# A spectral and state-space network on one core: long convolutions in quarter tiles of TensorE, the complex products summed by TensorE

## The chip, the cores and the metric

The kernel runs on one core of one Trainium2 chip. The metric is device time in microseconds. TensorE multiplies matrices and is recorded as PE, with its weight loads apart as PEld; VectorE is DVE, ScalarE is ACT, GpSimd is POOL, and SyncE (SP) mostly issues DMAs. Inputs, outputs and arithmetic are float32, except a few bfloat16 products that build the convolution kernels.

## The reference

Four layers with residuals on x of 1 x 2048 x 512, A, B, A, B; A filters with a 2-D FFT, B is a causal convolution over the 2048 positions with one kernel K per channel:

```python
def _A_ref(x, w_r, w_i):
    return irfft2(rfft2(x) * (w_r + 1j * w_i), s=(2048, 512))

def _B_ref(u, ...):
    dt = exp(log_dt); A = -exp(log_A_real) + 1j * A_imag; C = (C_real + 1j * C_imag) * dt[:, None]
    K = 2 * einsum("dn,dnl->dl", C, exp((A * dt[:, None])[:, :, None] * arange(2048))).real
    y = irfft(rfft(u.T, 4096) * rfft(K, 4096), 4096)[:, :2048].T
    return y + u * D_skip

x = x + _A_ref(layernorm(x)); x = x + _B_ref(layernorm(x)); x = x + _A_ref(layernorm(x)); x = x + _B_ref(layernorm(x))
```

The kernels K and their spectra are the same for both B layers.

## The kernel before

A B layer works in four blocks of 128 channels. For each block:

- `forward_b.rows` (four calls): the input's first Fourier stage. TensorE multiplies 64x64 pieces with a table T of twiddles; ACT copies the two banks to the tile z (L651).
- `turn` (eight calls): DVE transposes z in 32x32 pieces (L657), so that the position within a residue lies across partitions.
- `pair(i)` (four calls): the second stage. The weights are a matrix `mb` of 128 rows that is block-diagonal over two sets of channels, so half of each product is with zeros. It gives two planes, the real and the imaginary part.
- `weigh(i)`: the complex product with K's spectrum, two tiles `kk` of 128x512 per i. DVE makes four real products of 128x512 from PSUM into `wb` (L963), a small one mends frequency zero (L965), and four sums of 64x512 bring them together in the tile Y (`u`, L975). The strings YB and YC give each sum to POOL ("g") or DVE ("v").
- `back.units` (eight calls, four for each half j of Y): Y is the weight and MBT the moving operand, 16 products each; ACT copies to V (L988). The first call of each half also mixes frequency zero (L983, L984).
- `back.rows` (four calls): the last stage, 8 products each, and DVE adds the residual (L1002).

`kernel_time` builds K in time order for 32 channel groups (exponentials and sines on ACT, products on DVE at L840, L859 and L861, small products on TensorE at L872, a copy on ACT at L879 and stores `kt<-stage` at L883). `kernel_freq` then sends K through the same forward stages and keeps the spectrum in `kk` tiles, stored to memory (L938). The first B layer takes these tiles from SBUF directly (`kept`); the second loads them back (L957).

The order is written out by hand: lists of steps for one block, the next block's forward stages, K's build (`fill`) and the layer's tail are interleaved by position, and the framework's scheduler then sets each engine's stream. Each engine runs its stream in order. All matrix products of a group go through the helper `side_by_side`, whose one line is L319, and `mb`, `t` and `u` name the operands. In the first B layer PSUM has two banks for p1 and p3 together and three for p2 until K is built (`PM`), then five and three (`PB`); in the second two, three and three.

## Time and profile before

| what | value |
|---|---|
| median of 3 runs | 785.22 us (782.49 to 788.17) |
| profiled execution | 786.58 us, span 784.8 us |
| PE busy | 612.4 us, 8208 instructions |
| DVE busy | 646.6 us, 1301 instructions |
| ACT busy | 420.4 us |
| POOL busy | 415.4 us |
| moved by DMA | 80.26 MB |

A float32 product is two records in PE and two in PEld, so 64 products show as x128. From 120 us to 460 us the kernel builds K, beside the end of the first A layer and most of the first B layer; to about 540 us the rest of that layer runs; then the second A layer, and from 679 us the products of the second B layer.

### The profile page before, as it was taken

The page shows a single profiled execution, that of the slowest core. Times are in us where ns is not written, and L with a number is a line of the kernel's source. Part 1 is how long each engine was busy: PE and PEld are TensorE (multiplying, and loading weights), DVE is VectorE, ACT ScalarE, POOL GpSimd, SP SyncE. Part 2 cuts the span into 40 slices and gives each one's busy share as a digit, 9 for nine tenths or more (in the row PEclk, how much of TensorE's full clock was granted, in tenths as well). Part 3 has the DMA queues.
Part 4 walks back from the last instruction along what each step waited for, and adds up shares of the span by engine and source line. Part 5 has one row for each costly group of instructions (what it writes and reads, how often), then busy time and mean ns, then how long its engine had stood idle before and what let it go on. Part 6 is the DMA issues. An engine that isn't in the chain of part 4 may idle for free. (4 is left out here: it accounts for less than half of the span.)

```text
span 784.8 us, 20886 instructions
## 1 busy us (share of the span) xinstructions
PE 612.4 (78%) x8208; PEld 417.6 (53%) x8208; DVE 646.6 (82%) x1301; ACT 420.4 (54%) x919; POOL 415.4 (53%) x596
## 2 busy tenths in 40 slices
PE   3337788698758687897867977865899897889986
PEld 2336566464424342654343645644877664466666
DVE  7999749889997769968996977878587598789993
ACT  3434788755556676787477833323766335243322
POOL 3675886766625226732675166281055473375850
PEclk9656999998975999899989999997999898799998
DMA  8300651343547232452326359422122004134403
GB/s 320 117 0 1 147 124 49 102 101 129 125 161 148 72 105 49 129 139 79 43 67 146 113 120 252 133 82 81 54 82 83 28 14 147 56 91 128 145 24 105
DMA packets 144257, 80.26 MB, mean 102 GB/s; under 512 B 78656, under 2 KB 123840, under 8 KB 143264
## 3 DMA queue, kind: packets, MB, share of 16 engines
q1 hardware_dynamic: 143904, 78.51, 36.0%
q8 instruction: 65, 1.06, 0.5%
q0 software_dynamic: 256, 0.43, 0.3%
q14 instruction: 32, 0.26, 0.1%
HBM read 54.30 MB, written 25.03 MB: 101 GB/s over the span
## 5 line engine op out<-in xcount | busy, mean ns | idle before, releaser
L975 POOL TENSOR_TENSOR u<-wb,wb 64x512 f32<-64x512 f32 x90 | 137.0, 1523 | 81.2 <-DVE wb L963 74.5
L319 PE MATMUL p<-z,mb 128*64 128x512 f32 (+1 forms) x480 | 104.0, 543 | 13.2 <-DVE wb L963 5.8
L651 ACT COPY z<-p 128x512 f32<-128x512 f32 x96 | 51.5, 595 | 70.5 <-PE p L319 47.0
L861 DVE TENSOR_TENSOR qp<-qp,mag 128x1024 f32<-128x1024 f32 x64 | 83.3, 1305 | 1.2
L963 DVE TENSOR_TENSOR wb<-p,kk 128x512 f32<-128x512 f32 x128 | 80.6, 674 | 4.0 <-PE p L319 4.0
L859 DVE SCALAR_TENSOR_TENSOR qp<-qp,mag 128x256 f32<-128x256 f32 x128 | 63.6, 512 | 18.7 <-ACT qp L805 18.4
L319 PEld LDWEIGHTS p<-mb,u 128*64 128x64 f32 x2048 | 67.6, 146 | 17.9 <-issue 9.6
L319 PE MATMUL p<-mb,u 128*64 128x64 f32 x2048 | 69.9, 231 | 8.6 <-DVE u L975 4.2
L657 DVE STREAM_TRANSPOSE z<-z 128x512 f32<-128x512 f32 x96 | 58.5, 673 | 21.1 <-ACT z L651 21.1
L1087 POOL TENSOR_SCALAR w<-w,norms 128x128 f32<-128x128 f32 x64 | 37.8, 604 | 62.7 <-DMA w<-h 59.7
L530 DVE TENSOR_TENSOR w<-wt,p 128x514 f32<-128x514 f32 x64 | 42.5, 687 | 32.4 <-PE p L319 24.2
L535 POOL TENSOR_TENSOR w<-w,w 64x257 f32<-64x257 f32 x48 | 40.0, 834 | 53.7 <-DVE w L530 45.8
L872 PEld LDWEIGHTS pv<-qp 128*32 128x32 f32 x2048 | 38.0, 120 | 53.8 <-issue 20.2
L805 ACT ACTIVATE kf<-pk 128x512 f32<-128x512 f32 x64 | 38.8, 606 | 48.7 <-PE pk L841 48.4
L459 PE MATMUL p<-w,w 128*128 128x128 f32 x128 | 32.1, 429 | 40.6 <-DVE w L452 30.9
L319 PEld LDWEIGHTS p<-z,mb 128*64 128x64 f32 x480 | 34.4, 142 | 50.5 <-issue 30.9
L319 PE MATMUL p<-t,w 64*64 64x128 f32 x1024 | 48.1, 309 | 16.7 <-DMA w<-kt 8.1
L872 PE MATMUL pv<-qp 128*32 128x64 f32 x2048 | 51.6, 240 | 8.2 <-DVE qp L861 5.3
L988 ACT COPY u<-p 128x512 f32<-128x512 f32 x64 | 37.4, 589 | 38.1 <-PE p L319 38.1
L840 DVE TENSOR_SCALAR kw<-pk 128x512 bf16<-128x512 f32 x64 | 43.0, 679 | 13.3 <-PE pk L839 13.3
L319 PEld LDWEIGHTS p<-t,w 64*64 64x64 f32 x1024 | 36.8, 152 | 29.0 <-DMA w<-kt 10.7
L459 PEld LDWEIGHTS p<-w,w 128*128 128x128 f32 x128 | 27.8, 318 | 44.6 <-issue 24.7
(198 smaller groups left out, 1498.1 us busy)
## 6 DMA issues: line engine op xcount, KB each, us to landing
wt<-in_w SPq DMA_DIRECT2D x32, 257.0 KB
kf<-kk SPq DMA_DIRECT2D x32, 256.0 KB
kk<-kf SPq DMA_DIRECT2D x32, 256.0 KB
u<-in_x SPq DMA_DIRECT2D x16, 256.0 KB
hr<-in_x SPq DMA_DIRECT2D x16, 256.0 KB
kt<-stage SPq DMA_DIRECT2D x32, 128.0 KB
h<-hr SPq DMA_DIRECT2D x16, 256.0 KB
w<-kt SPq DMA_DIRECT2D x32, 128.0 KB
```

The source lines that it names most:

```text
L319: last = self.nc.tensor.matmul(out, weights, data, start=not more, stop=True, skip_group_check=True).ins
L459: nc.tensor.matmul(p[:, b], xf[:, b], t, start=True, stop=True)
L530: nc.vector.tensor_mul(m[pl], W, px[:, None, :].to_broadcast([128, 2, 257]))
L535: e[0].tensor_sub(Y[0:64, v], m[0][hs, 0], m[1][hs, 1])
L651: nc.scalar.copy(tiles["z"][:, :, :, b, m:m + 2].rearrange("p u j m r -> p (u j) (m r)"), ps[b].rearrange("p u j m r -> p (u j) (m r)"))
L657: nc.vector.transpose(tiles["zt"][:, u:u + 8].rearrange("p u j d -> p (u j d)"), tiles["z"][:, u:u + 8].rearrange("p u j b m r -> p (u j b ...
L840: nc.vector.tensor_scalar(whole, p, MAGIC, -MAGIC, op0=ALU.add, op1=ALU.add)
L859: nc.vector.scalar_tensor_tensor(QP[:, c, 0], QP[:, c, 1, :, ::-1], -1.0 if c else 1.0, m[:, 0], op0=ALU.mult, op1=ALU.mult)
L861: nc.vector.tensor_mul(t, t, mag[:, None, 1:3, 256 * j:256 * j + 256].to_broadcast([128, 2, 2, 256]))
L872: nc.tensor.matmul(p[32 * t:32 * t + 32, g], QP[:, c, 2, d], QP[:, c, 0:2, d], start=c == 0, stop=c == 1, tile_position=(0, 32 * t), skip_ ...
L963: nc.vector.tensor_mul(split(m[c, pl], "du", [32, 16]), by_channel(p), split(k[c], "du", [32, 16]))
L975: self.added = e[0].tensor_sub(y[0:64], v[0, 0], v[1, 1]), e[1].tensor_add(y[64:128], v[0, 1], v[1, 0])
```

## The change

- The channels of a block are split once more, into four sets of 32 (j, q). z has two sets in its lower 64 partitions and two in its upper, and every product of the convolution has 64 rows. `forward_b.rows` has 32 products of 64x32 weights instead of 16 of 64x64; `pair` has four products of 64x64 weights per kind, with no zeros; `units` is called four times, with two banks and 32 products for each plane M; `rows` is called twice, with two banks and 64 products of 64 columns.
- With ADD false (first B layer) DVE's four products per i go straight into two tiles M (`u`), times the spectrum's real part and times its imaginary part; nobody adds them. TensorE sums them in `units`, the second with turned weights (MT). With ADD true (second B layer) `pair` makes two kinds, one with turned weights (TWI); DVE makes four products per i into `wb`, and POOL adds them in two sums of 128x512 into one M.
- The spectrum is needed on other partitions: `weigh` loads four tiles per i, each in two DMAs that read every row twice, in both layers. Only the last block of the first B layer takes it from SBUF, with weights DUP. POOL copies frequency zero into the loaded tiles.
- M is a single set, written by a block's four `weigh` and read by its four `units`. `mix` comes once per block.
- DQ gives the stores `kt<-stage` and `kf<-kk` to ACT's queue instead of SP's. `stage` has one buffer instead of two, `qp` four instead of five, and LAGV is 3 instead of 4. `xw` has one buffer of twice the size.

```diff
@@ -19,14 +19,14 @@
-WW = 8
-DQ = ''
+WW = 6
+DQ = 'TaUa'
-LAGV = 4
+LAGV = 3
...
@@ -50,12 +50,13 @@
-QP = 5
+QP = 4
-WB = 7
-YB = 'vgggvggg'
-YC = 'vgggvgggvgvgvgvv'
+WB = 5
+ADD = False, True
+XW = 1
+WX = 11
...
@@ -638,13 +652,19 @@
                 tiles["z"] = self.sb("z", [64, 2, 2, 8, 2])
             xs = [src(n0 + i) for i in range(4)]
             ps = [self.ps("p1", [64, 2, 2, 2]) for b in range(2)]
...
+            products = []
+            e = extra() if extra and n0 == 0 else None
+            for m in range(2):
+                for j in range(2):
+                    for q in range(2):
+                        for c in range(2):
+                            for b in range(2):
+                                o = ps[b][64 * q + 32 * c:64 * q + 32 * c + 32, :, j, m]
+                                t = T[64 * b:64 * b + 64, n0 + 2 * m + c].rearrange("p (u r) -> p u r", r=2)
+                                d = slice(64 * j + 32 * q, 64 * j + 32 * q + 32)
+                                products.append((o, xs[2 * m + c][64 * b:64 * b + 64, d], t))
+                                if e is not None and m == c == b == 0:
+                                    products.append((o, e[:, d], t, True))
             self.side_by_side(products)
             m = n0 // 2
             for b in range(2):
@@ -657,23 +677,33 @@
             nc.vector.transpose(tiles["zt"][:, u:u + 8].rearrange("p u j d -> p (u j d)"),
                                 tiles["z"][:, u:u + 8].rearrange("p u j b m r -> p (u j b m r)"))
...
+        def pair(i, use, kinds):
+            z = tiles["zt"]
             last = None
...
+            for x, K in enumerate(kinds):
+                ps = [self.ps("p2", [512]) for q in range(2)]
                 products = []
...
+                for first in (1, 0) if i == 0 else (0,):
+                    us = slice(16 * i, 16 * i + 1) if first else slice(16 * i + (i == 0), 16 * i + 16)
+                    for j in range(2):
+                        for q in range(2):
+                            o = ps[q][64 * j:64 * j + 64].rearrange("p (u d) -> p u d", d=32)[:, us.start - 16 * i:us.stop - 16 * i]
+                            products.append((o, K[64 * q:64 * q + 64, 1 - first], z[64 * q:64 * q + 64, us, j]))
                 last = self.side_by_side(products, last)
...
+                for q in range(2):
+                    use(x, q, ps[q])
+        def first(kinds):
+            z = tiles["zt"]
+            ps = [self.ps("p2", [len(kinds), 32]) for q in range(2)]
+            self.side_by_side([(ps[q][64 * j:64 * j + 64, x], K[64 * q:64 * q + 64, 0], z[64 * q:64 * q + 64, 0, j])
+                               for x, K in enumerate(kinds) for j in range(2) for q in range(2)])
+            return ps
+        self.first = first
         return ([partial(rows, n0) for n0 in range(0, 16, 4)], [partial(turn, u) for u in range(0, 64, 8)],
                 [partial(pair, i) for i in range(4)])
@@ -918,95 +947,109 @@
         kn = {}
         rows, turns, pairs = self.forward_b(src, T, extra=skip)
+        first = self.first
         def keep(i):
...
+            k = [self.sb("kk", [512]) for q in range(2)]
+            def use(x, q, p):
+                nc.scalar.copy(split(k[q], "du", [32, 16]), by_channel(p))
+                self.dma("U")(kf[blk, i, q], k[q])
+            pairs[i](use, self.NAT)
+            if i == 0:
+                for q, p in enumerate(first(self.DUP)):
+                    nc.scalar.copy(self.kf0[:, blk, q], p)
+            if kept is not None and blk == 3:
+                kept[i] = k
         return rows, turns, [partial(keep, i) for i in range(4)]
...
+    def layer_b(self, kf, T, out, add, x=None, src=None, first=None, more=(), fill=(), switch=(), kept=None, fetch=None, after=None):
         nc = self.nc
         eng = self.adder
...
+        TBT = self.load("t2", "tbt", [2, 2, 16, 64])
+        M = [split(self.sb("u", [4096]), "qdu", [2, 32, 64]) for x in range(1 if add else 2)]
+        V = self.sb("u", [64, 2, 32])
+        def weigh(blk, pairs, i):
+            own = kept is not None and blk == 3
+            if own:
+                k = kept.pop(i)
+            else:
+                k = [[self.sb("kk", [512]) for q in range(2)] for x in range(2)]
+                for x in range(2):
+                    for q in range(2):
+                        for j in range(2):
+                            part = kf[blk, i, q][64 * j + 32 * x:64 * j + 32 * x + 32]
+                            part = bass.AP(tensor=part.tensor, offset=part.offset, ap=[[0, 2], *part.ap])
+                            self.dma("W")(k[x][q][64 * j:64 * j + 64], part)
+                        if i == 0:
+                            nc.gpsimd.tensor_copy(split(k[x][q], "du", [32, 16])[:, :, 0], self.kf0[:, blk, q, x])
             m = {}
...
+            def use(x, q, p):
+                p = by_channel(p)
+                for o in (x,) if own or add else range(2):
+                    y = M[o][:, q, :, 16 * i:16 * i + 16] if not add else split(self.sb("wb", [512]), "du", [32, 16])
+                    f = k[q] if own else k[o][q]
+                    nc.vector.tensor_mul(y, p, split(f, "du", [32, 16]))
+                    m[o, q] = y
+                if add and x == 1:
+                    eng.tensor_add(M[0][:, q, :, 16 * i:16 * i + 16], m[0, q], m[1, q])
+            pairs[i](use, self.DUP if own else [*self.NAT, *self.TWI] if add else self.NAT)
+        def mix():
+            p = self.ps("p3", [2, 32])
+            for q in range(2):
+                for x, m in enumerate(M):
+                    nc.tensor.matmul(p[:, q], self.MIX[:, x], m[:, q, :, 0], start=x == 0, stop=x == len(M) - 1,
+                                     skip_group_check=True)
+            nc.scalar.copy(M[0][:, :, :, 0], p)
+            if not add:
+                nc.gpsimd.memset(M[1][:, :, :, 0], 0.0)
         def back(blk):
...
+            def units(d):
+                ps = [self.ps("p3", [64, 8]) for j in range(2)]
+                self.side_by_side([(ps[j][64 * q:64 * q + 64, :, i], m[64 * j:64 * j + 64, q, d + i],
+                                    self.MT[64 * j:64 * j + 64, x], *[True] * x)
+                                   for i in range(8) for x, m in enumerate(M) for j in range(2) for q in range(2)])
+                for j in range(2):
+                    nc.scalar.copy(V[:, :, j, d:d + 8], ps[j])
             def rows(n0):
...
+                ps = [self.ps("p3", [8, 64]) for q in range(2)]
+                self.summed = self.side_by_side([(ps[q][64 * b:64 * b + 64, i], TBT[64 * q:64 * q + 64, r, b, n0 + i],
+                                                  V[64 * q:64 * q + 64, 32 * r + 16 * b + n0 + i].rearrange("p j d -> p (j d)"),
+                                                  *[True] * r)
+                                                 for i in range(8) for r in range(2) for q in range(2) for b in range(2)])
+                part = np.s_[:, n0:n0 + 8, 128 * blk:128 * blk + 128]
                 if src is not None:
...
+                    xs = self.sb("xw", [8, 128])
                     self.dma("X")(xs, src[part])
                     y = xs if self.h is None else self.h[part]
                 else:
                     y = xs = x[part]
...
+                for q, p in enumerate(ps):
+                    half = lambda t: t.rearrange("p n (j q d) -> p n j q d", j=2, q=2)[:, :, :, q]
+                    nc.vector.tensor_add(half(y), half(xs), p.rearrange("p n (j d) -> p n j d", j=2))
                 if src is None or self.h is None:
                     self.dma("O")(out[part], y)
                 if src is not None:
...
+                    for i in range(8):
                         nc.vector.bn_stats(self.stats[:, n0 + i, blk], y[:, i])
...
+            return [partial(units, d) for d in range(0, 32, 8)], [partial(rows, n0) for n0 in (0, 8)]
         steps = [first or self.forward_norm(0, T, src)] + [self.forward_norm(blk, T, src, "z3" if more and blk == 3 else "z")
                                                            for blk in range(1, 4)]
@@ -1015,18 +1058,18 @@
@@ -1015,18 +1058,18 @@
             chain.insert(at, (None, *m))
         if first is None:
             interleave(chain[0][1])
...
+            interleave(chain[0][2])
         last = []
         fill = [*fill, *[[]] * len(chain)]
         for i, (blk, _, _, pairs) in enumerate(chain):
             for at, f in switch:
                 if i == at:
                     f()
...
+            now, units, rows, special = pairs, [], [], []
             if blk is not None:
...
+                now = [partial(weigh, blk, pairs, i) for i in range(4)]
                 units, rows = back(blk)
+                special = [mix]
             then = chain[i + 1] if i + 1 < len(chain) else (None, [], [])
             tail = more and i == len(chain) - 3
             if tail:
@@ -1034,34 +1077,36 @@
                 then = chain[-1]
...
+            steps = [now[0], *last[:1], *special, now[1], *last[1:], now[2], *then[1][:2], now[3], *then[1][2:]]
+            turns = then[2]
+            for n in range(4):
+                steps += [*units[n:n + 1], *turns[2 * n:2 * n + 2]]
+            last = rows
             half = len(steps) // 2
             part = fill[i][:len(fill[i]) // 2], fill[i][len(fill[i]) // 2:]
             interleave(steps[:half], part[0])
             interleave(steps[half:], part[1])
             if tail:
                 keep = chain[-2][3]
...
                 interleave(chain[-2][1])
...
+                interleave(last)
+                interleave(chain[-2][2][:2])
                 fetch()
                 blk, _, _, pairs = chain[-1]
...
+                now = [partial(weigh, blk, pairs, i) for i in range(4)]
+                turns = chain[-2][2]
+                interleave([keep[0], *turns[2:4], now[0], keep[1], *turns[4:6], now[1], mix, keep[2], *turns[6:], now[2],
+                            keep[3], now[3]])
                 units, rows = back(blk)
...
+                interleave(units)
+                self.even = {}
                 for n0 in range(0, 16, 4):
                     for c, op in enumerate((nc.gpsimd.tensor_add, nc.gpsimd.tensor_sub)):
...
+                        self.even[c, n0] = self.sb("kk", [4, 128])
+                        op(self.even[c, n0], self.h[:, n0:n0 + 4, 0:128], self.h[:, n0:n0 + 4, 256:384])
+                last = rows
                 break
         if after:
             then = after()
@@ -1124,29 +1168,35 @@
-                                              qp=(6144, QP), kf=(2048, KF), stage=(4096, 2)))
+                                              qp=(6144, QP), kf=(2048, KF), stage=(4096, 1)))
-            outer.enter_context(net.phase("f", t=(16384, 1), z=(16384, 2), w=(2056, WB)))
-            outer.enter_context(net.phase("b", t2=(8192, 1), u=(16384, 2), kk=(2048, 8), ta="t2", wt="w", wb="w", xw="w"))
+            outer.enter_context(net.phase("z", z=(16384, 2)))
+            convolution = ExitStack()
+            convolution.enter_context(net.phase("f", t=(8192, 1), w=(2056, WB)))
+            convolution.enter_context(net.phase("b", t2=(16384, 1), u=(16384, 3), kk=(2048, 8), xw=(4096, XW), ta="t2", wt="w"))
-            net.small = net.load("mb", "mb", [512])
-            net.kc = net.load("kc", "kc", [2])
+            small = net.load("mb", "mb", [896])
+            net.NAT = [split(small[:, 0:128], "sm", [2, 64])]
+            net.DUP = split(small[:, 128:384], "sxm", [2, 2, 64])
+            net.DUP = [net.DUP[:, :, x] for x in range(2)]
+            net.TWI = [split(small[:, 384:512], "sm", [2, 64])]
+            net.MT = split(small[:, 512:640], "xm", [2, 64])
+            net.MIX = split(small[:, 640:896], "xm", [2, 128])
-                net.tags["wb"] = net.tags["xw"] = net.tags["w"]
-                folds.enter_context(net.phase("folds", side="right", tb=(8192, 1), fa=(4096, 2), xf=(8192, 2)))
+                folds.enter_context(net.phase("folds", side="right", tb="t", fa=(4096, 2), xf=(8192, 2), ts="w"))```

VectorE in the second B layer, the start of a block's weighing: `wb` are the products, `u` the sums, `p` banks of PSUM. Before:

```order
L963 TENSOR_TENSOR wb_9005<-p_1776_9002,kk_8998 128x512
L963 TENSOR_TENSOR wb_9007<-p_1776_9002,kk_8999 128x512
L975 TENSOR_TENSOR u_7827<-wb_8938,wb_8949 64x32x16
L963 TENSOR_TENSOR wb_9012<-p_1779_9009,kk_8998 128x512
L963 TENSOR_TENSOR wb_9014<-p_1779_9009,kk_8999 128x512
L975 TENSOR_TENSOR u_7827<-wb_9005,wb_9014 64x32x16
```

and after, around the transposes of the next block (L677) and the residual (L1045):

```order
L1002 TENSOR_TENSOR wb_10851<-p_1787_10845,kk_10833 128x512
L1002 TENSOR_TENSOR wb_10853<-p_1788_10846,kk_10834 128x512
L1002 TENSOR_TENSOR wb_10861<-p_1791_10855,kk_10835 128x512
L1002 TENSOR_TENSOR wb_10864<-p_1792_10856,kk_10836 128x512
L677 STREAM_TRANSPOSE z_10975<-z_10760 128x512 x8
L1045 TENSOR_TENSOR za_6525<-za_6525,p_1764_10657 128x8x2x32
```

Each product has a bank of its own, the sums are gone from VectorE's stream, and all eight transposes stand together.

ScalarE while K is built, before and after one store of K (`kt<-stage`; `pv` holds K's sums, `pk` the arguments of exponentials and sines). Only the changed kernel has the store on this engine:

```order
L909 COPY stage_2668<-pv_3366 128x64x2
L913 DMA kt<-stage_2668 2048x1x16 x4
L835 ACTIVATE mag_3453<-pk_3454 128x512
L835 ACTIVATE mag_3453<-pk_3460 128x512
L835 ACTIVATE kf_3469<-pk_3464 128x512
```

The four issues stand between a copy and the exponentials of the next channels.

SyncE while the second block of the first B layer is weighed, after the change (`kk<-kf` is the spectrum, `th<-parts` feeds K's build, `w<-kt` the next spectrum):

```order
L825 DMA th_4817<-parts 48x1x256 x2
L828 DMA th_4817<-parts 24x1x256 x6
L992 DMA kk_5256<-kf 64x1x512 x2
L992 DMA kk_5257<-kf 64x1x512 x2
L992 DMA kk_5258<-kf 64x1x512 x2
L992 DMA kk_5259<-kf 64x1x512 x2
L825 DMA th_4880<-parts 48x1x256 x2
```

The loads of the spectrum, which were not in this layer, stand ahead of loads for K's build on the same queue.

147 lines of the change are left out of this document (32 added, 115 removed).

## The prediction

> **What bounds the kernel now.** The profiled execution took 786.58 us for a span of 784.8 us, 1.4 us over the median of 785.22; I work in its time and subtract. I first cut the span into stages with the view of windows: K's build, the rest of the first B layer, the second A layer, and the second B layer's four blocks, each from its first weighing to the next one's. Columns: length; then busy time and count of PE, PEld, DVE, ACT and POOL; granted clock, DMA share, GB/s.
>
> ```profile
> 120.00:460.00 340.00, 270.46 (x4150) 158.22 (x4153) 295.13 (x569) 230.05 (x467) 175.85 (x222) 0.90 0.41 106
> 460.00:540.00 80.00, 58.24 (x1023) 43.35 (x1014) 63.66 (x119) 24.77 (x48) 44.43 (x43) 0.96 0.53 145
> 678.88:700.75 21.87, 18.68 (x316) 11.24 (x306) 20.28 (x31) 6.97 (x14) 16.59 (x12) 1.00 0.32 98
> 700.75:725.78 25.03, 23.54 (x479) 17.31 (x474) 22.54 (x34) 9.15 (x18) 16.69 (x12) 1.00 0.44 129
> 725.78:750.79 25.01, 23.55 (x462) 17.16 (x462) 23.47 (x35) 8.33 (x16) 16.59 (x12) 1.00 0.44 129
> 750.79:784.80 34.01, 25.86 (x542) 22.84 (x538) 20.84 (x30) 7.35 (x14) 12.48 (x9) 0.92 0.23 64
> ```
>
> In a middle block of the second B layer DVE works 22.5 and 23.5 of 25.0 us and PE as long: neither alone can be made faster for a gain. While K is built DVE works 295 of 340 us (87%), PE 80%, ACT 68%. The groups of instructions say what DVE does (first between 240 and 540 us, then in the two middle blocks), and its waits between 120 and 540 us what it lacks:
>
> ```profile
> L975 DVE TENSOR_TENSOR u<-wb,wb 64x512 f32<-64x512 f32 x19 | 21.6, 1135 | 0.2
> L934 DVE TENSOR_SCALAR kf<-kk,kc 64x32 f32<-64x32 f32 x8 | 3.2, 398 | 2.8 <-ACT kk L926 2.8
> L935 DVE SCALAR_TENSOR_TENSOR kf<-kk,kc,kf 64x32 f32<-64x32 f32 x8 | 3.0, 380 | 0.2
> L936 DVE TENSOR_SCALAR kk<-kk,kc 64x32 f32<-64x32 f32 x8 | 2.8, 349 | 0.0
> ...
> L963 DVE TENSOR_TENSOR wb<-p,kk 128x512 f32<-128x512 f32 x32 | 20.1, 677 | 3.7 <-PE p L319 3.7
> L975 DVE TENSOR_TENSOR u<-wb,wb 64x512 f32<-64x512 f32 x8 | 11.7, 1457 | 0.2
> L657 DVE STREAM_TRANSPOSE z<-z 128x512 f32<-128x512 f32 x16 | 9.9, 666 | 0.0
> L1002 DVE TENSOR_TENSOR za<-za,p 128x512 f32<-128x512 f32 x8 | 5.0, 663 | 0.0
> ...
> DVE qp L859 <- ACT qp L805: 18.4, 20, 2.3
> DVE z L657 <- ACT z L651: 16.5, 6, 4.5
> DVE kw L840 <- PE pk L839: 12.9, 6, 4.7
> ```
>
> A sum (L975) is the dearest per element: 1457 ns for 64x512 against 677 ns for a product of 128x512. And while K is built DVE's largest waits are for ACT, on which this change puts more.
>
> **TensorE's pace.** PE's bursts, with start, length and count, in the second B layer and, the last row, of K's sums:
>
> ```profile
> 702.40 3.95 PE L319 MATMUL p<-mb,u 128*64 128x64 f32 x128
> 711.18 2.84 PE L319 MATMUL p<-u,t 128*64 128x128 f32 x48
> 713.95 1.10 PE L319 MATMUL p<-t,x 64*64 64x128 f32 x32
> 709.79 1.08 PE L319 MATMUL p<-z,mb 128*64 128x512 f32 x4
> ...
> 447.15 0.65 PE L872 MATMUL pv<-qp 128*32 128x64 f32 x32
> ...
> L319 PE MATMUL p<-mb,u x2048: 219/222/369, 314.9 to 775.7; 128*64 128x64 f32 x187
> L872 PE MATMUL pv<-qp x2048: 216/219/316, 126.2 to 454.7; 128*32 128x64 f32 x187
> ```
>
> A lone record lasts 0.22 us for 64 columns, so starts are (3.95-0.22)/127 = 29 ns apart in `units`, where two 128x64 tiles lie side by side, and (0.65-0.22)/31 = 14 ns in K's sums, where four lie side by side. For the other forms I divide the burst less about 0.27 us: 27 ns in the first stage (four tiles), 54 ns in `rows` (two), some 215 ns for 512 columns (two). The pace follows columns divided by tiles. In the change `units` and `rows` have 64 columns in four tiles and the first stage 128 in eight: all come out at 14 ns, and `pair` at 107 ns.
>
> Records per block, before: units 256, rows 64, first stage 128, pair 32 of 512 columns: 256x29 + 64x54 + 128x27 + 32x215 ns = 7.4+3.5+3.5+6.9 = 21.3 us. After, in the second layer: 256+256+256 at 14 ns and 64 at 107 ns = 10.8+6.8 = 17.6 us, 3.7 less. In the first B layer units double (512): 14.3+3.4 = 17.7 us. A block of K's spectrum goes from 10.4 to 7.0. All three are gains.
>
> This holds if 14 ns is a pace of four tiles of any shape. The nearest other row, the first stage's 27 ns, has the same 64x64 tiles and loads the same 64 weight columns; K's sums load 32. I take 14 ns for the new forms, since both rows follow columns over tiles, and keep 27 ns as the other end. Trainium skill, "TensorE: Matmul & The Clock Gate", section "Wait — 56ns, not 53.3ns?", says starts never come closer than about 25 ns however few the columns. The burst of K's sums at 14 ns speaks against this as a limit here, unless its weights of 32 columns are the reason; by that rule the block would take the time of the first rival below.
>
> **Second B layer.** DVE per block after: 16 products x 0.677 + 8 transposes x 0.666 + 4 residuals x 0.663 = 10.8+5.3+2.7 = 18.8 us. The single M makes another cycle: POOL may write it only when the `units` of the block before have read it. The nearest rows are these (POOL's sums that go, a 128x512 sum of the A layer, and ACT's copy behind a call of units):
>
> ```profile
> L975 POOL TENSOR_TENSOR u<-wb,wb 64x512 f32<-64x512 f32 x90 | 137.0, 1523 | 81.2 <-DVE wb L963 74.5 <-DVE wb L965 1.4
> L1063 POOL TENSOR_TENSOR t<-za 128x512 f32<-128x512 f32 x8 | 11.1, 1420 | 0.1
> ...
> 690.06 0.59 ACT L988 COPY u<-p 128x512 f32<-128x512 f32 x1 [0.35 <-PE p L319]
> ```
>
> Eight sums are 11.4 to 12.2 us. A call of units is 64 records (0.9 us), then ACT's wait of 0.35 us and one copy of 0.59 before its bank is free: 4 x 1.84 = 7.4 us. The cycle is 18.8 to 19.6, level with DVE. DMA: loads double, 16 x 256 KB per block, and 1 MB of results:
>
> ```profile
> q1 hardware_dynamic: 11904, 10.49, 34.2%
> L957 SPq DMA_DIRECT2D kk<-kf x32: 319/320/1016, 644.1 to 739.7; - x32
> ```
>
> 10.49 MB at 34.2% in 105.9 us is 290 GB/s when busy, so 5.2 MB need 18 us; SP's 32 issues of 0.32 us are 10. Four things stand between 18 and 20 us. Before, DVE idled 1.5 to 2.5 us per block; I add 2 and take 20.9 us. Three periods: 71.9 to 62.7, 9.2 less. The last block: weighing and residuals 13.5, POOL's last two sums 2.8, units 7.4, rows 2 x 128 x 14 ns = 3.6, two residuals and a wait 1.7, and the last store to the end as now:
>
> ```profile
> 780.46 0.69 DVE za L1002
> ```
>
> 3.6 us, sum 32.6 against 34.0. Second layer: -11 us, between -18 (DVE alone sets it) and 0 (each cycle adds its waits, 24 us per block).
>
> **First B layer and K's build.** DVE loses the 21.6 us of sums, 9.0 of mending, and half of L965 (1.6): 32 us, half of it before 460 us. POOL loses half of its 90 sums, which were in nobody's way in this layer. I count DVE's 16+16 us at its shares of 87% and 80%, since where it waits its own work is not what is late: 27 us, if nothing new comes late. New is:
>
> ```profile
> L883 SPq DMA_DIRECT2D kt<-stage x32: 558/1030/2817, 155.3 to 462.8; - x32
> L938 SPq DMA_DIRECT2D kf<-kk x32: 319/336/2322, 271.7 to 516.4; - x32
> L859 DVE SCALAR_TENSOR_TENSOR qp<-qp,mag 128x256 f32<-128x256 f32 x128 | 63.6, 512 | 18.7 <-ACT qp L805 18.4
> L861 DVE TENSOR_TENSOR qp<-qp,mag 128x1024 f32<-128x1024 f32 x64 | 83.3, 1305 | 1.2
> ```
>
> ACT issues 32 stores of 1.03 us and 32 of 0.34: 44 us in 340 where it has 110 free. Queued behind each group of four (4.1 us) are K's exponentials and sines, and DVE waits for these. DVE's cover is the `qp` tiles ahead, each 2 x 0.51 + 1.3 + 0.68 = 3.0 us of its work, and there are four now, not five; I let a quarter through, 11 us. The two banks of p1 are both taken by one call of units or rows, so that PE stands for two copies (1.2 us) and the hand-over: 6 calls x 1.5 us x 2 blocks = 18 us of PE, which has 70 us idle there; I let 3 us through. The loads `kk<-kf` wait on SP for products and hold up loads for K behind them; `xw` has one buffer, so a load waits for a store. I charge 2 us for both; bounds are 0 and 20, with no row for them. Sum: -27+11+3+2 = -11 us. The second A layer keeps its work.
>
> 786.6-11-11 = 764.6, less 1.4: 763 us. Own range 747 to 776: nothing new comes late in the first layer (-27-11), or half of its 11 us is left and the second's blocks take 23 us (-6-3).
>
> **Rivals.** (1) *PE keeps 27 ns per record.* Four 64x64 tiles of 64 columns go no faster than of 128. For: that first-stage row with its 64 weight columns. Against: 14 ns in K's sums. Then a block of the second layer has 512x27 + 256x14 + 6.8 = 24.2 us of PE, as long as today's 25, and units and rows at its end are longer: about 0 there. In the first layer units and rows take 20.7 where they took 10.9, 39 us of PE over four blocks, less 24 for `pair` (three blocks and four spectra at 3.4): 15 us more of PE in place of less, each of its bursts twice as long before DVE and ACT can go on. I take DVE's gain as lost to that: 780 to 792, middle 785.
>
> (2) *Slower: ACT's issues hold K's build.* The place is ACT between 130 and 460 us. If every store stops DVE's supply and PE's 18 us come through too, 33+11+18 = 62 us stand against 27 of gain: +35-11 = +24, 809 us. It decides where more than 38 of the 62 us reach DVE and costs over 1% from 46 on, that is, where the look-ahead of `qp` is under two tiles (6 us) when a group of four stores, with its wait for free buffers, comes. For: the 18.4 us of waits for ACT, the most DVE has, and the shorter look-ahead. Against: those waits are at most 2.3 us each. Half of the 62 us gives 778.
>
> (3) *The first layer shows all its gain and the second its -18*: 786.6-27-18 = 741.6, less 1.4, 740. It needs ACT's issues to be hidden wholly.
>
> **How the numbers follow.** Chances: forecast 0.50, (1) 0.20, (2) 0.20, (3) 0.10. Within 1%, about what a measurement can tell from no change, is 777 to 793. Faster: forecast and (3) nearly whole, a little of (1), 0.60. Same: most of (1), the mild part of (2), 0.22. Slower: the rest, 0.18. Predicted is 763. The range goes from 742, with half of (3) outside, to 793, without the worse part of (2).
>
> **What would show it.** PE bursts of units at 14 ns and a period near 21 us in the second layer: right. Starts 27 ns apart: rival 1. ACT in its queue at `kt<-stage` for over 4 us with DVE idle at L859's successor: rival 2. If POOL or DMA ends the waits of the second layer, the charge of 2 us per block was too small. The prediction falls if the time before 460 us grows, or if periods stay at 25 us though PE has the pace.

## The result and the profile after

The changed kernel takes 1284.49 us (median of 4 runs) against 786.33 for the kernel before (4 runs on the same chip): 1.635 times as long, 95% interval 1.623 to 1.647. The profiled execution has a span of 1284.2 us. The forecast was 763 us. Here and below times are medians of all runs, while ratios leave out slow runs, those over 1.5% longer than the fastest of their kernel: among the experiments below one of e5's four, one of g1's (1114.66 us) and two of h3's.

Two rows of one view, the tile of a normalization's result, cut both traces into three stages: the second A layer begins with the first of ACT's scalings (`ts<-tb,lnn`; `kk<-tb,lnn` in the kernel before) and ends with the last of its sixteen `x<-za,lnn`. Columns: min, median and max ns, then first and last start. The kernel before:

```profile
L485 ACT ACTIVATE kk<-tb,lnn x16: 385/399/427, 543.2 to 557.6; 128x128 f32<-128x128 f32 x16
L615 ACT ACTIVATE x<-za,lnn x16: 798/800/815, 644.3 to 669.1; 128x512 f32<-128x512 f32 x16
```

The changed kernel:

```profile
L499 ACT ACTIVATE ts<-tb,lnn x16: 386/402/414, 808.1 to 829.5; 128x128 f32<-128x128 f32 x16
L629 ACT ACTIVATE x<-za,lnn x16: 797/800/814, 912.1 to 935.2; 128x512 f32<-128x512 f32 x16
```

Up to the second A layer 543 us have become 808 (+265), the A layer has kept its 126 to 127, and the second B layer has gone from 784.8 - 669.1 = 116 to 1284.2 - 935.2 = 349 us (+233). The B layers, which the change is about, hold all of it. The waits between 240 us and the end say what they lack (us in total, times, longest):

```profile
POOL kk L994 <- DMA kk<-kf: 302.8, 24, 65.2
PEld p L333 <- issue: 209.2, 139, 25.4
ACT u L1028 <- PE p L333: 184.5, 26, 38.0
DVE u L1002 <- DMA kk<-kf: 179.1, 26, 14.0
POOL e L856 <- ACT mag L835: 174.5, 12, 66.7
DVE wb L1002 <- DMA kk<-kf: 154.3, 35, 6.0
```

VectorE stands 179 us in the first B layer and 154 in the second for loads of the spectrum, `kk<-kf`, and GpSimd 303 us for the same loads. The view of transfers of the second B layer from 1000 us on (40 equal slices, busy share of the 16 engines in tenths, and GB/s):

```profile
DMA  1111111111111131131111111131131111115102
GB/s 50 50 50 50 52 52 50 53 53 50 50 50 50 50 114 55 55 118 51 53 53 50 50 56 50 50 116 49 51 119 52 52 50 53 50 50 159 51 2 77
...
kk<-kf SPq DMA_DIRECT2D x94, 128.0 KB
```

This is no idle queue. It is a queue that is always at work and holds 50 GB/s: a tenth of the engines' time is busy, slice after slice, and the slices above 110 GB/s hold stores of the results, which SP issues at 1102, 1120, 1184, 1206 and from 1248 us on. Counted from the trace's packets on this queue, in some 40 of the 50 us from 1205 on exactly two packets are under way. Two engines of sixteen are a share of 0.125. The chain of waits of that stretch is nearly all loads (start, length):

```profile
1214.28 9.85 DMA kk<-kf
1224.16 0.05 DVEq L1002
1224.21 0.04 issue
1224.26 0.70 DVE wb L1002
1224.95 0.71 SPq L992
1225.66 0.05 issue
1225.71 14.07 DMA kk<-kf
```

And two blocks of the second B layer, each from its first long burst of units to the next one's, in the view of windows (length; busy time and count of PE, PEld, DVE, ACT, POOL; granted clock; DMA share; GB/s):

```profile
1029.17:1115.72 86.55, 34.99 (x798) 18.76 (x793) 17.26 (x28) 7.77 (x15) 10.67 (x12) 0.64 0.15 57
1115.72:1200.25 84.53, 38.12 (x847) 20.61 (x851) 18.36 (x29) 8.86 (x17) 10.70 (x12) 0.62 0.17 62
```

A block loads 16 x 256 KB = 4.19 MB in 84.5 us: 50 GB/s. The forecast was a period of 20.9 us. VectorE's own work in a block is 17.3 and 18.4 us, as forecast (18.8).

### The profile page after: what moved, and what is told of

Its sections match the earlier page's. It is cut to its first block, busy times and chain, and to the rows that moved or that the text cites. A ratio compares the mean times of both kernels' runs of the same rounds, so it can differ in the third digit from the quotient of the medians.

```text
span 1284.2 us, 29841 instructions
## 1 busy us (share of the span) xinstructions
PE 716.5 (56%) x12600; PEld 448.3 (35%) x12600; DVE 594.8 (46%) x1223; ACT 420.1 (33%) x919; POOL 324.6 (25%) x570
## 3 DMA queue, kind: packets, MB, share of 16 engines
q1 hardware_dynamic: 82960, 89.18, 21.6%
## 5 line engine op out<-in xcount | busy, mean ns | idle before, releaser
L333 PE MATMUL p<-z,mb 64*64 64x512 f32 (+2 forms) x744 | 162.0, 671 | 191.1 <-DVE u L1002 112.5
L1002 DVE TENSOR_TENSOR wb<-p,kk 128x512 f32<-128x512 f32 x64 | 43.0, 688 | 253.4 <-DMA kk<-kf 154.3
L1002 DVE TENSOR_TENSOR u<-p,kk 128x512 f32<-128x512 f32 x64 | 42.2, 687 | 221.2 <-DMA kk<-kf 179.1
L333 PE MATMUL p<-mb,u 64*64 64x64 f32 x3072 | 71.3, 245 | 109.4 <-POOL u L1005 67.0
L333 PEld LDWEIGHTS p<-z,mb 64*64 64x64 f32 x744 | 37.0, 169 | 246.9 <-issue 124.5
L333 PEld LDWEIGHTS p<-mb,u 64*64 64x64 f32 x3072 | 64.9, 157 | 123.0 <-POOL u L1005 69.5
L1028 ACT COPY u<-p 128x512 f32<-128x512 f32 x64 | 34.4, 589 | 184.6 <-PE p L333 184.5
L994 POOL COPY kk<-kf 128x32 f32<-128x32 f32 x28 | 7.8, 283 | 307.8 <-DMA kk<-kf 302.8
L677 DVE STREAM_TRANSPOSE z<-z 128x512 f32<-128x512 f32 x96 | 58.3, 674 | 28.7 <-ACT z L671 28.7
L835 ACT ACTIVATE mag<-pk 128x512 f32<-128x512 f32 x64 | 36.3, 600 | 103.3 <-DMA kt<-stage 59.5
L333 PE MATMUL p<-t,w 64*32 64x128 f32 x2048 | 54.6, 320 | 15.0 <-ACT z L671 9.1
L1005 POOL TENSOR_TENSOR u<-wb,wb 128x512 f32<-128x512 f32 x32 | 39.9, 1266 | 89.4 <-DVE wb L1002 60.3
L856 POOL TENSOR_TENSOR e<-mag 128x16 f32<-128x16 f32 x32 | 11.8, 370 | 191.7 <-ACT mag L835 182.9
L544 DVE TENSOR_TENSOR w<-wt,p 128x514 f32<-128x514 f32 x64 | 42.4, 686 | 32.9 <-ACT w L528 10.1
L835 ACT ACTIVATE kf<-pk 128x512 f32<-128x512 f32 x64 | 39.2, 612 | 49.0 <-PE pk L871 48.7
## 6 DMA issues: line engine op xcount, KB each, us to landing
kk<-kf SPq DMA_DIRECT2D x224, 128.0 KB
kt<-stage ACTq DMA_DIRECT2D x32, 128.0 KB
w<-kt SPq DMA_DIRECT2D x32, 128.0 KB
```

Source lines behind the costliest of these rows:

```text
L333: last = self.nc.tensor.matmul(out, weights, data, start=not more, stop=True, skip_group_check=True).ins
L544: nc.vector.tensor_mul(m[pl], W, px[:, None, :].to_broadcast([128, 2, 257]))
L677: nc.vector.transpose(tiles["zt"][:, u:u + 8].rearrange("p u j d -> p (u j d)"), tiles["z"][:, u:u + 8].rearrange("p u j b m r -> p (u j b ...
L835: last["x"] = nc.scalar.activation(*a, **k).ins
L1002: nc.vector.tensor_mul(y, p, split(f, "du", [32, 16]))
L1005: eng.tensor_add(M[0][:, q, :, 16 * i:16 * i + 16], m[0, q], m[1, q])
```

## Experiments

Labels with e work on the changed kernel (e2 on the kernel before), f on a version of it that stores the spectrum doubled, g and h on the kernel before (h3 on the changed one). There are four runs of each (two of e2, ten of h4), and ratios are to the kernel before with 95% intervals. In e2, e5, e6 and h3 the loads bring other rows of the spectrum than are needed, so that only their times mean something.

**What the loads cost.** In the changed kernel a load fills 64 rows from 32, each 32 rows twice: the access pattern `[0, 2], 32 rows, 512` has two steps outermost. My theory was that the outermost step is what is dealt out to the DMA engines. Rivals: twice the bytes, or the number of issues. In e1 the doubled load is two loads of 32 rows:

```diff
-                            part = bass.AP(tensor=part.tensor, offset=part.offset, ap=[[0, 2], *part.ap])
-                            self.dma("W")(k[x][q][64 * j:64 * j + 64], part)
+                            for h in range(2):
+                                self.dma("W")(k[x][q][64 * j + 32 * h:64 * j + 32 * h + 32], part)
```

> The changed kernel with each doubled load split in two DMAs of 32 rows, one for each copy; same rows, same bytes into SBUF, 448 issues instead of 224. Theory (a load whose outermost step is 2 is carried by 2 of the 16 DMA engines, 51 GB/s): the loads spread over 16 engines, the waits for them go, and the time falls from 1284 us to the forecast's 747 to 790 us; SP's issues (64 x 0.32 us = 20 us per block of the second B layer) may hold a few us. Rival bytes (each row read twice, 104 MB in place of 80): nothing changes, 1250 us or more. Rival issues (SP's count of DMAs is what is late): slower than 1284 us, since they double.

Measured: 948.53 us, 1.206 (1.198 to 1.214). The same bytes and twice the issues take 336 us off, so neither bytes nor issues made the 1284. But it is far above the 747 to 790 that I expected. Its transfers from 660 to 860 us (the second B layer begins at 775, slice 24) run at twice to three times the 50 GB/s:

```profile
GB/s 0 53 5 260 55 109 104 69 95 106 68 94 54 0 0 3 0 0 58 65 3 105 381 91 147 109 136 122 121 134 142 120 116 125 121 139 89 199 96 60
```

e2 gives the kernel before the doubled form, in the second B layer alone, with its own number of bytes:

```diff
-                self.dma("W")(k[c], kf[blk, i, c])
+                for j in range(2):
+                    part = kf[blk, i, c][64 * j:64 * j + 32]
+                    part = bass.AP(tensor=part.tensor, offset=part.offset, ap=[[0, 2], *part.ap])
+                    self.dma("W")(k[c][64 * j:64 * j + 64], part)
```

> The kernel before with one edit: in the second B layer each spectrum tile is loaded in two DMAs that read 32 rows twice (the tile then holds other rows, and the time is read for the loads alone). Theory of two engines: 8 tiles of 256 KB per block at 51 GB/s are 41 us where a block took 25, so three periods grow by 48 us and the last block by 10 to 16 us: 840 to 855 us. Rivals (bytes, or anything in the quarter tiles or their sums): the same bytes reach SBUF, 780 to 795 us.

Measured: 849.59 us, 1.080 (1.070 to 1.091), inside the theory's 840 to 855. Its transfers between 660 and 860 us show the same plateau:

```profile
DMA  2511111111111111111111441111111443500700
GB/s 85 195 53 50 49 53 53 50 50 53 53 51 50 50 53 50 50 53 51 57 50 50 134 149 50 51 53 53 50 50 50 142 140 92 141 3 20 193 0 0
```

The form of the pattern sets 50 GB/s, in a kernel that is otherwise the one before. (No run separates the count of 2 from the step of zero that makes the second copy; the two packets under way speak for the count.) e5 loads 128 plain rows at a time, 112 loads of 256 KB in place of 224 of 128 KB:

```diff
-                        for j in range(2):
-                            part = kf[blk, i, q][64 * j + 32 * x:64 * j + 32 * x + 32]
-                            part = bass.AP(tensor=part.tensor, offset=part.offset, ap=[[0, 2], *part.ap])
-                            self.dma("W")(k[x][q][64 * j:64 * j + 64], part)
+                        self.dma("W")(k[x][q], kf[blk, i, q])
```

> The changed kernel with each spectrum tile loaded by one plain DMA of 128 rows (not the right rows; same bytes into SBUF, 112 loads of 256 KB). Theory of two engines: 740 to 785 us, and what it is faster than the split loads of 32 rows is the price of their issues. Rival bytes: 1250 us or more.

Measured: 889.02 us, 1.131 (1.120 to 1.141), again far above the 740 to 785 that I expected. So of the 498 us the loads make 1284 - 889 = 395: 336 for the form with the outermost step of 2, and 59 more (e1 less e5) for 448 loads of 32 rows in place of 112 of 128. Whether these 59 are the short rows or the number of issues stays open, for in e1's second B layer SP does hardly anything but issue:

```profile
859.58 27.62 SPq L992 DMA_DIRECT2D kk<-kf  x48
```

48 loads of 64 KB in 27.62 us are 114 GB/s, the rate of the slices above. In the same layer of e5, SP stands 62.6 us for tiles to come free. About 100 us are left with loads of the form that they had before. e3 is e1 with all stores issued by SP again (`DQ = ''`):

> As the split loads of 32 rows, and the stores of K and of its spectrum back on SP's queue. If ACT's issues hold K's build (rival 2 of the prediction), 10 to 40 us faster than with the split loads alone; if they lie in ACT's idle time, within 8 us of it or slower, since SP's queue is longer.

Measured: 942.28 us, 1.199 (1.192 to 1.206): 6 us under e1. ACT's issues are not the 100 us, at least not where SP has to take them up beside e1's 448 loads.

**Where the 100 us lie.** The same two rows for e5:

```profile
L499 ACT ACTIVATE ts<-tb,lnn x16: 385/402/415, 623.5 to 644.6; 128x128 f32<-128x128 f32 x16
L629 ACT ACTIVATE x<-za,lnn x16: 797/801/814, 724.4 to 747.5; 128x512 f32<-128x512 f32 x16
```

The first B layer is 80 us late (623.5 against 543.2), the second takes 886.3 - 747.5 = 139 us instead of 116. Its waits between 275 and 510 us, while K is built:

```profile
DVE xw L1042 <- PE p L333: 26.6, 3, 10.1
DVE xw L1042 <- DMA xw<-h: 7.8, 1, 7.8
ACT mag L835 <- DMA kt<-stage: 21.6, 4, 5.9
POOL e L856 <- ACT mag L835: 58.2, 11, 8.7
POOL kk L991 <- DMA kk<-kf: 46.1, 6, 27.4
POOL u L1015 <- PE p L1011: 17.4, 1, 17.4
```

Many places, none dominant. I tried the undoing of single ones first. f1 makes the doubled spectrum with TensorE's doubled kinds and stores it twice, so that loads are plain and right, and GpSimd has nothing to mend in them for blocks 0 to 2:

```diff
-            pairs[i](use, self.NAT)
+            pairs[i](use, self.NAT if own else self.DUP)
...
-                self.dma("U")(kf[blk, i, q], k[q])
+                    self.dma("U")(kf[blk, i, x, q], k[x][q])
```

> The spectrum of the kernel (blocks 0 to 2) is made doubled by TensorE (the kinds with both halves of the rows alike) and written twice, so that each load is one plain 128-row transfer of 256 KB with the right rows; GpSimd then has no column to mend in what was loaded, except in block 3. Theory: of the 100 us that the plain loads of wrong rows (889 us) still stood over the kernel before, a good half is GpSimd held behind loads and behind the mixing of column 0 while K is built; without the mending some 45 to 64 us of its waits go and K's build ends 20 to 40 us earlier, 850 to 870 us. Rival (the rest is ACT's and SP's issues): 24 more copies of 0.59 us and 24 more stores of 0.33 us on ACT, 22 us, make it 890 to 910.

Measured: 931.76 us, 1.181 (1.173 to 1.189). GpSimd's waits for loads while K is built are gone, and the time is 43 us over e5: the theory fell. It is above the rival's 890 to 910 too: it has 24 more copies and 48 more stores on ACT (block 3 is stored in four pieces where I had counted none), and each quarter that is kept takes four tiles `kk` instead of two. Which of these makes the 43 us no run separates. f2 is f1 with the zeros of M's column 0 written by ACT:

```diff
-                nc.gpsimd.memset(M[1][:, :, :, 0], 0.0)
+                nc.scalar.activation(M[1][:, :, :, 0], p, ACT.Copy, scale=0.0)
```

> As the kernel with two copies, and the zeros of M's column 0 are written by ACT (a copy of the mixed column times zero) instead of GpSimd. Theory: GpSimd stood 39 us for this while K was built, with K's magnitudes queued behind it; 10 to 25 us less than the two copies alone. Rival (GpSimd's wait is covered, SP's queue or the banks set the pace of the first B layer): within 5 us of it.

Measured: 932.02 us, 1.181 (1.174 to 1.188): nothing. GpSimd's wait behind the mixing was covered. Next the banks. A kind of products now fills two banks of PSUM, of which p2 has three; f3 gives it four after K's build, at p1's and p3's cost:

```diff
-PB = [5, 3]
+PB = [4, 4]
...
-                outer.enter_context(net.phase("pc", P, p1=(2048, 2), p2=(2048, 3), p3=(2048, 3)))
+                outer.enter_context(net.phase("pc", P, p1=(2048, 2), p2=(2048, 4), p3=(2048, 2)))
```

> As the kernel with zeros on ACT, and after K is built and in the second B layer the kinds of products have four banks of PSUM, not three (4 and 4 instead of 5 and 3; 2, 4 and 2 instead of 2, 3 and 3). Theory: a kind fills two banks, so with three TensorE and VectorE take turns; with four the second B layer's block takes 22 to 25 us instead of 30 and the end of the first B layer is some 10 us shorter: 25 to 35 us less. Rival (the one M and GpSimd's sums set the block's period): blocks of 28 to 30 us, less than 8 us less.

Measured: 917.94 us, 1.163 (1.156 to 1.169): 14 us less, half of what I expected. By the two rows of its trace the first B layer ends 13 us earlier than in f2 and the second takes 10 less, while the second A layer, which has lost a bank, takes 6 more. So the banks bind in both B layers. f4 is f3 with two M and no sums on GpSimd in the second B layer too (`ADD = False, False`):

> As the kernel with four banks, and the second B layer in the form of the first: two M, the products written straight to them, no sums on GpSimd, 512 records of units per block instead of 256. If GpSimd's sums and the one M set the period, blocks go to 20 to 23 us and the time is 10 to 30 us less than with four banks alone; if VectorE's products and the hand-over of banks set it, it stays within 6 us; if TensorE sets it (3.6 us more of units per block), it is 10 to 15 us more.

Measured: 942.72 us, 1.194 (1.186 to 1.202): 25 us more than f3, which is more than any of the three named. By its rows the second B layer takes 152 us where f3's takes 131. The sums on GpSimd were the cheaper way.

**Putting the suspects into the kernel before.** Undoing one of many limits shows little when another stands behind it. So the other way round: each new scarcity alone, in the kernel before.

```diff
g1  QP 5 -> 4, LAGV 4 -> 3, WB 7 -> 5, stage=(4096, 2) -> (4096, 1)
g2  k = [self.sb("kk", [512]) for c in range(4)], each loaded from kf, in the first B layer, blocks 0 to 2
g3  ps = [self.ps("p3", [64, 4]) for h in range(2)] in units, [2, 128] twice in rows, first B layer
g4  g1 + g2 + g3
h1  xw="w", later xw=(2048, 4) -> xw=(2048, 1)
h2  g4 + h1 + DQ = 'TaUa'
```

> The kernel before with the changed kernel's smaller buffers and look-ahead while K is built: four tiles qp (five before), total three steps behind (four), one stage (two), five w in the first B layer (seven). Theory: the changed kernel's groups of K units were already 22 us late at 275 us, before the first load of a spectrum, and ACT stood 41 us at the one stage; the smaller buffers alone cost 20 to 45 us (808 to 833 us). Rival (the buffers are deep enough either way, the loads and banks do it): under 8 us.

> The kernel before, and the first B layer loads the spectrum of blocks 0 to 2 back from memory, four plain loads of 256 KB per quarter of a block, as the changed kernel does, where the kernel before keeps it in place: 48 loads more. Theory: the loads wait for the spectrum's stores and for free tiles at the head of SP's queue and hold K's own loads behind them: 15 to 35 us more. Rival (they are hidden, as I had charged them with the single xw at 2 us): under 5 us.

> The kernel before, and in the first B layer each call of units and rows spreads over two banks (half of the columns in each), so that while K is built every call takes both banks of p1, as in the changed kernel; ACT and VectorE read it in two instructions. Theory: TensorE's queue stands at each call for two reads, 10 to 20 us more. Rival (the 3 us that I had charged): 0 to 6 us.

> The kernel before with all three: smaller buffers, the round trip of the spectrum and two banks per call. If these three make the first B layer's loss, the second A layer begins 55 to 85 us later than in the kernel before and the time is 840 to 870 us; under 820 would mean that the rest lies in the quarter tiles themselves (the order of the steps, the second weighing of each product).

> The kernel before with a single tile for the residual of the first B layer (xw of its own, one of 128x512, where it shared seven, and later had four). Theory: VectorE stands in its own queue for rows and for xw (34 us in the changed kernel with plain loads, K's terms behind it), and SP stands for the store from xw: 8 to 20 us more. Rival (a load waits for a store beside other work): under 4 us.

> The kernel before with small buffers, the round trip of the spectrum, two banks per call (the three together: 843 us, second A layer from 584 us instead of 543), one xw, and the stores of stage and spectrum issued by ACT. The changed kernel with plain loads begins its second A layer at 623 us. If these five are the whole of the first B layer's loss it begins at 610 to 625 us here too (868 to 885 us in all); if the quarter tiles themselves (two kinds' banks of one kind, the mixing, GpSimd's waits) hold the rest, at 584 to 600 us.

| in the kernel before | time, us | ratio (interval) | second A layer begins |
|---|---|---|---|
| nothing | 788 to 789 | 1 | 543.2 |
| g1, small buffers | 814.38 | 1.027 (1.018 to 1.036) | 555.6 |
| g2, round trip of the spectrum | 799.99 | 1.013 (1.008 to 1.018) | 553.6 |
| g3, two banks per call | 805.02 | 1.019 (1.013 to 1.025) | 557.2 |
| g4, these three | 843.06 | 1.068 (1.062 to 1.073) | 583.9 |
| h1, one xw | 827.17 | 1.045 (1.039 to 1.052) | 581.1 |
| h2, all five | 884.94 | 1.119 (1.112 to 1.126) | 621.7 |

(The start of the second A layer moves by some us without a cause ahead of it: 547.1 in e2, which changes the second B layer alone.) Each one costs, and the rival of each single run (under 4 to 8 us) fell. g1 and g3 lie in the theory's range, g2 with 11 us under it and h1 with 39 us far over it. g4's time is as expected, its second A layer begins 41 us late, less than the 55 that I had set for "all". The row of h2 beside that of e5 above:

```profile
L485 ACT ACTIVATE kk<-tb,lnn x16: 386/394/414, 621.7 to 640.3; 128x128 f32<-128x128 f32 x16
L615 ACT ACTIVATE x<-za,lnn x16: 797/800/824, 742.9 to 767.6; 128x512 f32<-128x512 f32 x16
```

With all five, the kernel before begins its second A layer 78 us late, the changed kernel with plain loads 80. So shortages of this kind are enough for a loss of this size, without any quarter tile. That they are the loss of the changed kernel is not shown, for they are not the same shortages and the engines wait elsewhere. In g1 and h2 the five w also hold the products `wb`, which the changed kernel does not make in this layer; g3 has twelve calls per block on two banks where the changed kernel has six; h1's xw has half the size. Between 275 and 510 us of h2 GpSimd stands 51.6 us for products at its sums (L981), of which the changed kernel has none there, and VectorE 5.8 us at xw, where e5 has 26.6 and 7.8. (That the whole times also agree, 885 and 889, is chance: the five w of g1, g4 and h2 go on into the second A layer, which takes 15 to 20 us longer there and not in e5, while e5 loses 23 us in the second B layer.)

Two runs on the changed kernel then tried to get the first layer's share back. h3 has one M there as in the second layer, and spends the 16 KB on buffers (`ADD = True, True`; five qp, look-ahead four, two stages, two xw, six w):

> The changed kernel with plain loads (of wrong rows, so its products are of other numbers; times only) and one M in the first B layer as in the second, with sums on GpSimd: the 16 KB that this frees give back five qp, a look-ahead of four, two stages, two xw and six w. Theory (buffers cost most of what is left): the second A layer begins at 575 to 600 us instead of 623, 840 to 866 us in all. Rival (four kinds per quarter in three banks, and sums before K's magnitudes on GpSimd, cost what the buffers give): 880 to 900 us.

Measured: 899.98 us, 1.129 (1.117 to 1.140), the rival's 880 to 900. Its second A layer begins at 625.8 us, no earlier than e5's. GpSimd now waits 122 us for VectorE's products between 240 and 620 us. Either the buffers were bought back with sums and banks, or they were not what was short; this run cannot tell. e6 splits the one xw of e5 into two of half the size:

```diff
-            return [partial(units, d) for d in range(0, 32, 8)], [partial(rows, n0) for n0 in (0, 8)]
+            return [partial(units, d) for d in range(0, 32, 8)], [partial(rows, n0) for n0 in range(0, 16, w)]
...
-            convolution.enter_context(net.phase("b", t2=(16384, 1), u=(16384, 3), kk=(2048, 8), xw=(4096, XW), ta="t2", wt="w"))
+            convolution.enter_context(net.phase("b", t2=(16384, 1), u=(16384, 3), kk=(2048, 8), xw=(2048, 2 * XW), ta="t2", wt="w"))
```

> The changed kernel with plain loads (wrong rows of the spectrum, times only), and the memory of the one xw as two tiles of half the size: rows is called four times a block for 4 columns each, not twice for 8, and a load may run beside the residual before it. One xw put into the kernel before cost 39 us. If it is the single tile as such (a load behind a store, VectorE and SP standing for both), 10 to 30 us less than the 889 us of the plain loads; if VectorE stands for TensorE's rows (26.6 of its 34 us of waits at the residual) and not for the tile, or calls of half the size take both banks as often as they gain, within 6 us or more.

Measured: 891.29 us, 1.134 (1.125 to 1.142), the same as e5. Its second A layer does begin 11 us earlier (612.9 against 623.5), but ends only 4 us earlier, and the second B layer is 4 us longer. Between 275 and 510 us VectorE's wait for the load of xw is gone, and it stands 38.3 us at the residual for TensorE's rows in place of 26.6: there it stands mostly for TensorE, not for the tile. So in the kernel before the cost of the five is shown; what makes the 80 us of the changed kernel's first B layer stays open.

h4, the kernel before with nine w (`WB = 9`), asked whether its own ring was short:

> The kernel before with nine tiles w instead of seven. Seven less two cost the small buffers 14 us in the second A layer alone; if the ring is still short at seven, 3 to 8 us less than the kernel before; if seven cover it, within 1%.

Measured: 788.73 us, 1.000 (0.996 to 1.003). Seven cover it. No version here beats the kernel before.

**The second B layer.** In e5, GpSimd's first sums of the second, third and fourth block, and the four calls of units between the second and third:

```profile
795.42 7.44 POOL L1002 TENSOR_TENSOR u<-wb,wb 128x512 f32<-128x512 f32 x6
821.54 4.98 POOL L1002 TENSOR_TENSOR u<-wb,wb 128x512 f32<-128x512 f32 x4 [15.90 <-PE p L333]
849.39 5.00 POOL L1002 TENSOR_TENSOR u<-wb,wb 128x512 f32<-128x512 f32 x4 [14.51 <-PE p L333]
```

```profile
809.26 1.33 PE L333 MATMUL p<-mb,u 64*64 64x64 f32 x60 [1.92 <-DVE za L1042]
813.96 1.21 PE L333 MATMUL p<-mb,u 64*64 64x64 f32 x66
817.41 1.09 PE L333 MATMUL p<-mb,u 64*64 64x64 f32 x58
820.20 1.16 PE L333 MATMUL p<-mb,u 64*64 64x64 f32 x64
```

GpSimd's sums stand 15.9 and 14.5 us for the units of the block before, so the one M does close a cycle, as the prediction had it, but it takes 26.1 and 27.9 us, not 18.8 to 19.6 (and 34.6 from the first block to the second). It is not the only bound, since f3's fourth bank took 10 us off this layer; and no run has a second set of M. The four calls of units begin 2.8 to 4.7 us apart, not 1.84, since TensorE takes products and the next block's first stage between them: 809.3 to 821.4 is 12 us where 7.4 were charged. VectorE's waits from 749 to 860 us say why the sums come late as well:

```profile
DVE wb L999 <- PE p L333: 29.0, 22, 2.9
```

It waits 22 times for TensorE's products, of which three banks hold one kind and a half.

## Why the prediction was wrong, step by step

**The step that failed: "10.49 MB at 34.2% in 105.9 us is 290 GB/s when busy, so 5.2 MB need 18 us."** The 290 GB/s came from loads of 128 plain rows; the change's loads have another access pattern, which the diff shows. They ran at 50 GB/s, so a block's 4.2 MB took 84 us and not 18 with the results included. e1, e2 and e5 show it: the form alone makes 336 of the 498 us, its replacement by plain loads takes off 395. The diff was enough to ask for a row of the same pattern, and there was none in the trace of before; both ends of the cost should have been kept, and no upper end for DMA stood in the sum or in the range. A rule that speaks against the change was overlooked as well. The Trainium skill, "DMA: Bandwidth & Descriptors", section "Rules for kernel authors", says that the engines of a transfer are set by its slowest dimension that is not 1, and names a leading zero-stride broadcast of c copies as confined to at most c engines. This case's trace agrees: two packets under way, 50 GB/s, share 0.1. Weighed beside the 290 GB/s, that rule would have made a slower rival.

**"I charge 2 us for both; bounds are 0 and 20, with no row for them"** (the first layer's loads and the single xw). In the changed kernel the 48 tiles of 256 KB that this layer loads are 12.6 MB, some 250 us at 50 GB/s, and with plain loads (e5) 185 of its 265 us go. Put singly into the kernel before, the round trip with plain loads costs 11 us and one xw (of half the size) 39: the charge was 2 where these two measured 50, and the upper bound 20 was too low as well.

**The two banks of p1, "I let 3 us through":** g3 measured 16, in the kernel before and with twice as many calls on two banks. That this is near the 18 us that I had counted is in part luck, since the calls are not the same; the cover of "70 us idle" did not hold there. The Trainium skill, "TensorEngine Tiling (Array Packing)", section "Gotcha 1: PSUM Pressure", says that row tiling raises the pressure on PSUM, as different row tiles write to different banks; f3's 14 us for one bank more is in line with it.

**A term that was missing:** four qp in place of five and the shorter look-ahead appeared only as cover for ACT's stores, and stage and w had no term in the sum. Small buffers put into the kernel before delay the first B layer by 12 us.

**ACT's issues of stores, 11 us:** e3 measured 6. Rival 2 had its sign right and its mechanism wrong. ACT did stand in its queue for `kt<-stage` (21.6 us in e5), but taking the stores off ACT gave little, and in the kernel before they add nothing: g4's delay of 41 us and h1's of 38 already make the 78 of h2, which has ACT's stores besides.

**DVE's -27 us in the first layer:** its work went down (594.8 us busy in the whole span, 646.6 before), but with plain loads the layer still ends 80 us later. I read this as a chain that four engines hand round, in which the share of a single engine's time is not what is late; no run takes it apart.

**TensorE's pace was right.** A burst of rows in e5, and one of units in the list above:

```profile
825.37 2.10 PE L333 MATMUL p<-u,t 64*64 64x64 f32 x128
```

(2.10 - 0.22)/127 = 14.8 ns, and for units (1.16 - 0.22)/63 = 14.9; 14 was forecast. Rival 1 falls. The rule of the Trainium skill that the prediction weighed ("TensorE: Matmul & The Clock Gate", starts never under about 25 ns) does not hold here for four tiles side by side. But the sum made of this pace, 17.6 us of TensorE per block in place of 21.3, did not come. Two periods of e5's second B layer (length; then busy time and count of PE, PEld, DVE, ACT and POOL; granted clock; DMA share; GB/s):

```profile
795.42:821.54 26.12, 22.49 (x739) 14.13 (x735) 15.56 (x25) 6.80 (x14) 10.22 (x11) 0.93 0.53 162
821.54:849.39 27.85, 24.59 (x730) 16.06 (x726) 17.54 (x28) 6.67 (x14) 10.68 (x13) 0.88 0.63 189
```

PE is busy for 22.5 and 24.6 us, as long as in a block before (23.5). The sum counts the distance of starts in long bursts, while here units, products and first stage come in turns, in bursts as short as one record of 0.63 us; how much of the busy time is waiting within PE the trace does not tell. So the shorter spacing did not shorten TensorE's busy time per block. (One reading of the rows before does not come out either: four records of 512 columns in 1.08 us, less 0.27, are 270 ns apart, not 215.)

**The second layer's "add 2 and take 20.9":** the cycle was named rightly as one bound, and the term "4 x 1.84 = 7.4" for units was mis-sized, 12 us in place, because it priced the calls as if TensorE had nothing between them; the three banks for two-bank kinds had no term. With plain loads this layer takes 139 us in place of 116, so that even there the change would have lost: the sign of the forecast was wrong without the loads too.

**What was to show it** did: the time before 460 us grew, and DMA ended the second layer's waits. The range of 742 to 793 missed because it was built from TensorE's, VectorE's and ACT's bounds only.

## What to carry to other kernels

A transfer is priced by a row of the same access pattern, not of the same bytes: look at the size of its outermost step before anything else, and where the trace has no such row, keep both ends. A change that takes memory is priced by what it takes it from: four small scarcities that looked hidden cost 11 to 39 us each, put alone into a pipeline that hands work round four engines, while undoing a single one in the changed kernel showed next to nothing. Two kernels that are late by the same amount need not be late for the same reason: compare where they wait, too. A wait that is large in the table, as GpSimd's behind the mixing of column 0, may still be covered; only its removal tells.

## What the runs showed of the hardware

- Loads whose outermost step is 2 moved 50 GB/s, in two kernels, with two packets under way. Loads of 32 rows held 109 to 147 GB/s through most of e1's second B layer (above), with SP issuing them one behind the other. Plain loads of 128 rows, with the stores of results, reach 200 to 260 GB/s in many slices of e5's second B layer (749 to 886 us):

```profile
GB/s 5 0 157 81 227 159 239 231 148 103 208 224 240 86 139 259 153 5 246 216 160 171 261 158 259 91 89 241 188 237 49 134 153 5 0 7 5 0 156 155
```

- Records in four 64x64 tiles side by side start 14.8 ns apart for 64 columns of f32, with 64 weight columns each (128 records in 2.10 us).
- The granted clock was lower where TensorE was less busy: 0.64 and 0.62 in the two blocks shown of the changed kernel, where PE is busy 35 of 87 and 38 of 85 us, against 1.00 in the middle blocks before (23.5 of 25), with 0.736 over the whole span (0.899 before).
